# Two passes over the feed-forward slices become three, and VectorE takes the casts of q, k, v and x

## The chip, the cores and the metric

One core of one Trainium2 chip runs the whole program in one launch. The metric is the device time of that launch in microseconds (us). The core has TensorE for matmuls (PE, its weight loads are PEld), VectorE (DVE), ScalarE (ACT) and GpSimd (POOL); SyncE (SP) issues every DMA here. Each engine works through its own list of instructions in a fixed order and waits where an operand isn't there yet.

## The reference

```python
def phi(x):                                   # q and k: 8 batches, 8 heads, 576 tokens, 64 wide
    proj = x @ w_phi                          # 64 -> 128 features
    proj = proj - max(abs(proj), axis=-1)     # one number for each token
    return concat([exp(proj), exp(-proj)])    # 256 features
q_p, k_p = phi(q), phi(k)
kv = k_p.T @ v                                # (256, 64) for each head
z = k_p.sum(tokens)
x = (q_p @ kv) / (q_p @ z + 1e-6)             # heads side by side: 4608 tokens, 512 wide
out = ((x @ w_a) * (x @ w_b)) @ w_out         # 512 -> 1536 -> 512
```

q, k, v and w_phi are float32; the three feed-forward weights are 64-bit floats.

## The kernel before

**Number formats.** A float32 matmul costs TensorE several passes over its columns. The kernel therefore splits most operands into a high part in `float32r` (`hi`, a cast) and a low part (`lo`, source minus high part) and adds three products, hi·hi + hi·lo + lo·hi. The helper `split` issues the cast on one engine and the subtraction on VectorE. The first head pairs of the program are "plain": their float32 operands go to TensorE unsplit. `PLAIN_K, PLAIN_Q, PLAIN_KV, PLAIN_NUM` say up to which of the 32 pairs this holds in the k projection, the q projection, the product of features and v, and the numerator.

**Attention.** Heads go in 32 pairs. A pair has four chunks of 128 tokens and half a chunk that it shares with its neighbour. `features` projects a chunk of k: the tokens are the weights of the matmul and the feature matrix streams past in 256 columns. Plain pairs stream a block-diagonal matrix `wk32`, so that one matmul does both heads. Split pairs stack high part and low part of one head in the 128 rows (`stack`), which takes one matmul for each head and chunk, and then a copy `kb` on ScalarE and an add `kd` on VectorE to join the halves (L236, L237). The absolute maximum (`m`), the subtraction (`kd`), two exponentials (`ke`) and the split `keh`, `kel` follow; `kv_add` accumulates `kvps`. `k_finish` transposes `kvps`. `q_side` does the same for q with features on partitions: projection `pq`, copy to `p`, an all-reduce of the absolute maximum over partitions on GpSimd (L350), subtraction, exponentials `qe`, split `qeh`, `qel`, and the numerator matmuls `pn` with the denominator as 65th row. Numerators go to DRAM (`xun`), denominators are inverted (`reciprocals`) and go to DRAM as `rec`.

**Feed-forward.** The 1536 inner columns are 12 slices of 128. Pass one (`moe_block`) does 6 slices for 16 blocks of 288 tokens and writes partial sums to `part` in DRAM. A block's x is the product of `xun` and `rec` (L533), split into `xh`, `xl`. Pass two (`second_pass`, `winograd`) does the other 6 slices for 9 blocks of 512 tokens, two slices and four quarters of 128 rows of x at a time, with seven products in place of eight; it needs sums of weights (`load_factors`) and sums of x (`factors_of_x`) that VectorE makes. It adds `part` and writes the output. The 64-bit weights are decoded on ScalarE and VectorE (`decode`).

**Order of the work.** `attention_steps` gives every step of a pair a turn; after each turn `run(work, int(due))` lets steps of feed-forward blocks run, `PACE0` and later `PACE` steps a turn, so that their matmuls fill TensorE while attention goes on. When the turns are over, 5 blocks of pass one are left (`BLOCKS_LAST`); beside them the weights of pass two are made. A timeline scheduler then sets the final order on each engine. PSUM has 8 banks: `ps_moe` 3, attention 4 and `kvacc` 1; after attention `ps_late` has 5 beside `ps_moe`.

Of the kernel before, what the change touches and what calls it, by code (L numbers as in the profile page):

```python
# [59 lines left out]
def tile_kernel(ctx, tc, qT, km, kr, vm, vr, w_phi, w_a, w_b, w_out, out):  # L60
# [95 lines left out]
    def k_load(b, pr, a1, a2, ps, consts, st):  # L156
# [4 lines left out]
        if i < PLAIN_K:  # L161
            k32 = a1.tile([P, n], F32, tag="ks", bufs=2, name=f"k32_{u}")
            nc.sync.dma_start(k32, km[b, pr])
        else:
            k32 = a1.tile([P, 2, n], F32, tag="k32", name=f"k32_{u}")
            for r in range(2):
                nc.sync.dma_start(k32[r * D : (r + 1) * D], km[b, pr].rearrange("(j d) s -> d j s", j=2))
# [21 lines left out]
    def rest_load(b, g, a1, a2, ps, consts, st):  # L189
# [3 lines left out]
        if i < PLAIN_K:  # L193
            k32 = a1.tile([P, P], F32, tag="rk32", name=f"rk32_{u}")
            nc.sync.dma_start(k32, kr[b, g])
        else:
            k32 = a1.tile([P, 2, P], F32, tag="rk32", name=f"rk32_{u}")
            for r in range(2):
                nc.sync.dma_start(k32[r * D : (r + 1) * D], kr[b, g].rearrange("(j d) s -> d j s", j=2))
# [18 lines left out]
    def features(u, i, k_, c0, n, a2, ps, consts):  # L218

        wk32, wk2 = consts[3:5]  # L220
        d = a2.tile([P, 4, F], F32, tag="kd", bufs=1, name=f"kd_{u}")[:, : 2 * n]
        if i < PLAIN_K:
            pk = ps.tile([P, 2, 2 * F], F32, tag="att", name=f"pk_{u}")
            for c in range(n):
                nc.tensor.matmul(pk[:, c], k_[:, (c0 + c) * P : (c0 + c + 1) * P], wk32, start=True, stop=True)
# [616 lines left out]
```

## Time and profile before

| what | value |
|---|---|
| median of 3 runs | 1262.51 us (1260.01 to 1264.18) |
| profiled execution, span from first to last instruction | 1260.6 us |
| granted TensorE clock, mean | 0.998 |
| TensorE busy | 1229.8 us (98%) |
| VectorE busy | 928.8 us (74%) |
| ScalarE busy | 734.3 us (58%) |
| GpSimd busy | 157.3 us (12%) |
| DMA | 138.24 MB, mean 110 GB/s |

The page gives no time of its own for the profiled execution beside the span; the three runs lie within 3.6 us of that span. TensorE's busy share overstates its use, since the matmuls overlap in the records; how far apart they start tells what one costs. The page's slices show TensorE and VectorE both well filled until about 680 us, where attention ends, and VectorE half idle after it.

### The profile page before, as it was taken

The page shows a single profiled execution, that of the slowest core. Times are in us where ns is not written, and L with a number is a line of the kernel's source. Part 1 is how long each engine was busy: PE and PEld are TensorE (multiplying, and loading weights), DVE is VectorE, ACT ScalarE, POOL GpSimd, SP SyncE. Part 2 cuts the span into 40 slices and gives each one's busy share as a digit, 9 for nine tenths or more (in the row PEclk, how much of TensorE's full clock was granted, in tenths as well). Part 3 has the DMA queues.
Part 4 walks back from the last instruction along what each step waited for, and adds up shares of the span by engine and source line. Part 5 has one row for each costly group of instructions (what it writes and reads, how often), then busy time and mean ns, then how long its engine had stood idle before and what let it go on. Part 6 is the DMA issues. An engine that isn't in the chain of part 4 may idle for free.

```text
span 1260.6 us, 22965 instructions
## 1 busy us (share of the span) xinstructions
PE 1229.8 (98%) x8588; PEld 1131.8 (90%) x8588; DVE 928.8 (74%) x1682; ACT 734.3 (58%) x1577; POOL 157.3 (12%) x70
## 2 busy tenths in 40 slices
PE   7889999999999999999999999999999999999998
PEld 4556789899999999999999999999999999999997
DVE  6989658898898989989974983599556556456443
ACT  5766668788888889988885542454223223233221
POOL 2232221221222212221220000000000000000000
PEclk9999999999999999999999999999999999999999
DMA  7665443443444435344233561142432332331221
GB/s 188 174 182 154 117 125 90 108 128 103 122 110 123 127 101 141 81 129 130 62 82 104 166 204 58 46 146 83 125 94 70 107 101 67 101 103 51 66 68 50
DMA packets 126287, 138.24 MB, mean 110 GB/s; under 512 B 39712, under 2 KB 92448, under 8 KB 126176
## 3 DMA queue, kind: packets, MB, share of 16 engines
q1 hardware_dynamic: 126176, 136.78, 38.4%
q8 instruction: 67, 1.10, 0.4%
q14 instruction: 44, 0.36, 0.1%
HBM read 108.12 MB, written 28.61 MB: 108 GB/s over the span
## 4 chain that ended last, share of the span: by engine, by line
PE 76%; DVE 9%; DMA 6%; ACT 5%; issue 2%; SPq 1%; POOL 0%; DVEq 0%; ACTq 0%
PE pab L648 21%; PE po L695 11%; PE pa L565 10%; PE pb L565 10%; PE po L588 9%; PE kvps L292 6%; PE pn L370 5%; PE pq L346 2%; DMA raw_b<-in_w_b 1%; PE pk L234 1%; DVE qs L154 1%; DMA rb<-rec 1%; DMA r<-den 1%; DVE kd L240 1%; DVE kel L149 1%
## 5 line engine op out<-in xcount | busy, mean ns | idle before, releaser
L350 POOL PARTITION_ALL_REDUCE mb<-p x64 | 156.6, 2448 | 495.9 <-ACT p L347 465.8
L565 PE MATMUL pb<-xh,wh_b 128*128 128x288 f32 x384 | 114.9, 299 | 2.9 <-ACT h L569 2.9
L565 PE MATMUL pa<-xh,wh_a 128*128 128x288 f32 x384 | 115.5, 301 | 0.4 <-ACT o L591 0.2
L565 PE MATMUL pb<-xh,wl_b 128*128 128x288 f32 x384 | 114.5, 298 | 0.0
L565 PE MATMUL pa<-xh,wl_a 128*128 128x288 f32 x384 | 114.4, 298 | 0.0
L142 ACT CAST hh<-h 128x288 fp32r<-128x288 f32 (+1 forms) x150 | 72.7, 503 | 70.7 <-DVE h L570 40.7
L565 PE MATMUL pa<-xl,wh_a 128*128 128x288 f32 x384 | 113.2, 295 | 0.0
L565 PE MATMUL pb<-xl,wh_b 128*128 128x288 f32 x384 | 112.7, 293 | 0.0
L588 PE MATMUL po<-hh,wl_o 128*128 128x288 f32 x384 | 112.4, 297 | 0.0
L588 PE MATMUL po<-hl,wh_o 128*128 128x288 f32 x384 | 111.9, 295 | 0.3 <-DVE hl L149 0.3
L588 PE MATMUL po<-hh,wh_o 128*128 128x288 f32 x384 | 110.3, 298 | 0.6 <-DVE h L570 0.6
L149 DVE TENSOR_TENSOR hl<-h,hh 128x288 fp32r<-128x288 f32 (+1 forms) x150 | 81.2, 554 | 22.7 <-ACT hh L142 22.5
L695 PE MATMUL po<-hl,wh_o 128*128 128x512 f32 x216 | 84.5, 391 | 0.0
L695 PE MATMUL po<-hh,wl_o 128*128 128x512 f32 x216 | 84.3, 390 | 0.0
L533 DVE TENSOR_TENSOR x<-x,rb 128x288 f32<-128x288 f32 (+1 forms) x100 | 56.0, 564 | 37.8 <-DMA x<-xun 26.2
L695 PE MATMUL po<-hh,wh_o 128*128 128x512 f32 x216 | 79.2, 392 | 0.0
L565 PEld LDWEIGHTS pb<-xh,wh_b 128*128 128x128 f32 x384 | 72.2, 188 | 5.0 <-ACT h L569 3.9
L565 PEld LDWEIGHTS pa<-xh,wh_a 128*128 128x128 f32 x384 | 72.2, 188 | 3.8 <-issue 2.3
L588 PEld LDWEIGHTS po<-hl,wh_o 128*128 128x128 f32 x384 | 72.5, 189 | 1.1 <-DVE hl L149 0.7
L565 PEld LDWEIGHTS pa<-xl,wh_a 128*128 128x128 f32 x384 | 72.9, 190 | 0.6 <-issue 0.2
L565 PEld LDWEIGHTS pa<-xh,wl_a 128*128 128x128 f32 x384 | 72.1, 188 | 1.3 <-issue 1.1
L565 PEld LDWEIGHTS pb<-xl,wh_b 128*128 128x128 f32 x384 | 72.8, 190 | 0.3
(226 smaller groups left out, 3793.7 us busy)
## 6 DMA issues: line engine op xcount, KB each, us to landing
q<-in_qT SPq DMA_DIRECT2D x110, 144.0 KB
k<-in_km SPq DMA_DIRECT2D x55, 256.0 KB
xun<-xn SPq DMA_DIRECT2D x64, 144.0 KB
x<-xun SPq DMA_DIRECT2D x64, 144.0 KB
rb<-rec SPq DMA_DIRECT2D x128, 72.0 KB
part<-o SPq DMA_DIRECT2D x16, 576.0 KB
o<-part SPq DMA_DIRECT2D x36, 256.0 KB
out_x<-o SPq DMA_DIRECT2D x36, 256.0 KB
```

The costliest lines, as they stand in the source:

```text
L142: eng.copy(dst, src)
L149: eng_lo.tensor_tensor(lo, src, hi, op=ALU.subtract)
L154: eng_lo.tensor_tensor(hi_lo[D:], src[D:], hi_lo[D:], op=ALU.subtract)
L292: nc.tensor.matmul(st["kv_ps", b, pr][:width, j], v_[:, j, :width], e_[:, j], start=(left == NFULL and j == 0 and n_ == 0), stop=(left == ...
L346: nc.tensor.matmul(pq[:, :HALF], w_, q_[:, tok], start=(n_ == 0), stop=(n_ == len(parts) - 1))
L350: nc.gpsimd.partition_all_reduce(mb, p32, P, bass_isa.ReduceOp.absmax)
L370: nc.tensor.matmul(pn[: D + 1, :HALF], kv_[:, 2 * j + s, :], e_[:, s, tok], **at)
L533: nc.vector.tensor_tensor(x32, x32, rb, op=ALU.mult)
L565: nc.tensor.matmul(acc, w[:, cc * P : (cc + 1) * P], x, start=(k == 0), stop=(k == 3 * NCC - 1))
L588: nc.tensor.matmul(acc, w[:, cc * P : (cc + 1) * P], h, start=(k == 0), stop=(k == 3 * NFS[p] - 1))
L648: nc.tensor.matmul(acc[to][:, i], w_, x_, skip_group_check=True, **at)
L695: nc.tensor.matmul(acc[cc], w[:, cc * P : (cc + 1) * P], h, **at)
```

## The change

Three passes of 4 slices take the place of two of 6. Pass one runs in 9 blocks of 512 tokens, and the other two passes both use the seven-product form, with two groups of two slices for each block (`later_passes`). Pass one writes its normalised x to DRAM (`xnorm`), and the later passes read that in place of `xun` and `rec`. The weights of pass three are made during pass two; those that have no room are written to DRAM (`keep`) and fetched into the places of pass two's weights behind its last block (`fetch`).

In attention the split k projection uses the block-diagonal form: three matmuls of 256 columns for each chunk, and no join. The first 5 pairs are plain in place of 9 (7 in place of 11 for `kvps`). The casts of k, v, q and x go from ScalarE to VectorE. The tiles `qs`, `qe`, `qeh`, `qel` and `kd` have two buffers. `k_finish` is cut into two steps. PSUM is 2 banks for `ps_moe`, 5 for attention and 1 for `kvacc`, and later 6 + 2.

```diff
-PACE0, PACE, PACE0_UNTIL = 0.65, 0.9, 18
+PACE0, PACE, PACE0_UNTIL = 0.6, 0.62, 18
-PLAIN_K, PLAIN_Q, PLAIN_KV, PLAIN_NUM = 9, 9, 11, 9
+PLAIN_K, PLAIN_Q, PLAIN_KV, PLAIN_NUM = 5, 5, 7, 5
-    "k_hi": "vss",
+    "k_hi": "vvv",
-    "v_hi": "sss",
+    "v_hi": "vvv",
-    "q_hi": "vss",
+    "q_hi": "vvv",
-SLICES0 = 6
-T2 = 512
-BLOCKS_LAST, AHEAD = 5, 0.7
+SLICES = (4, 4, 4)
+T1, T2 = 512, 512
+BLOCKS_LAST, AHEAD, LATER = 2, 2.5, 0.75
+LATE, EXTRA = 19, 7
...
-    ps_moe = ctx.enter_context(tc.tile_pool(name="ps_moe", bufs=3, space=PSUM))
+    ps_moe = ctx.enter_context(tc.tile_pool(name="ps_moe", bufs=2, space=PSUM))
-    part = dpool.tile([DM, NT], F32, name="part")
+    parts = [dpool.tile([DM, NT], F32, name=f"part{i}") for i in range(2)]
+    xnorm = dpool.tile([DM, NT], F32, name="xnorm")
-        ps = c.enter_context(tc.tile_pool(name="ps_att", bufs=4, space=PSUM))
+        ps = c.enter_context(tc.tile_pool(name="ps_att", bufs=5, space=PSUM))
...
 # k_load
-            ks = a1.tile([P, 2, n], F32R, tag="ks", bufs=2, name=f"ks_{u}")
-            stack(ks, k32, engine("k_hi", b), engine("k_lo", b))
+            kh, kl = (a1.tile([P, n], F32R, tag=f"k{p}", bufs=2, name=f"k{p}_{u}") for p in "hl")
+            split(kh, kl, k32, engine("k_hi", b), engine("k_lo", b))
...
 # features
-            for c in range(n):
-                pk = ps.tile([P, 2, 2, F], F32, tag="att", name=f"pk_{u}_{c}")
-                for j in range(2):
-                    nc.tensor.matmul(pk[:, j], k_[:, j, (c0 + c) * P : (c0 + c + 1) * P], wk2, start=True, stop=True)
-                to = slice(2 * c, 2 * c + 2)
-                nc.scalar.copy(kb[:, to], pk[:, :, 1])
-                nc.vector.tensor_tensor(d[:, to], pk[:, :, 0], kb[:, to], op=ALU.add)
+        parts = products(k_, (wk32,) if len(k_) == 1 else wks)
+        for c in range(n):
+            tok = slice((c0 + c) * P, (c0 + c + 1) * P)
+            for n_, (x_, w_) in enumerate(parts):
+                at = dict(start=(c == n_ == 0), stop=(n_ == len(parts) - 1))
+                nc.tensor.matmul(pk[:, c], x_[:, tok], w_, skip_group_check=True, **at)
...
 # load_x
-            split(xh, xl, x32, nc.scalar, nc.vector)
+            split(xh, xl, x32, nc.vector, nc.vector)
...
+    def put(key, shape, places, stored):
+        name = "_".join(map(str, key))
+        if stored is None:
+            pool, tag = slots[key] = places.popleft()
+            return pool.tile(shape, F32R, tag=tag, name=f"w_{name}")
+        fetches[key] = dpool.tile(shape, F32, name=f"wd_{name}")
+        return stored["pool"].tile(shape, F32R, tag="stage", bufs=2, name=f"ws_{name}")
+    def fetch(key, place):
+        pool, tag = place
+        t = pool.tile(list(fetches[key].shape), F32R, tag=tag, name="w_" + "_".join(map(str, key)))
+        nc.sync.dma_start(t.bitcast(F32), fetches[key])
+        weights[key] = t
...
 # moe_block, pass one
+            if f == 1:
+                for c, x_ in enumerate(xs):
+                    nc.sync.dma_start(xnorm[c * P : (c + 1) * P, j * T : (j + 1) * T], x_[2])
...
 # factors_of_x, passes two and three
-            x = [x_chunk(1, j, cc, pool, 4) for cc in (c, c + NCC // 2)]
+            for i in range(2):
+                cc = c + i * NCC // 2
+                nc.sync.dma_start(x[i], xnorm[cc * P : (cc + 1) * P, j * T2 : (j + 1) * T2])
...
-    def second_pass(xin):
+    def later_passes(xin, after):
+        blocks = [(p, j) for p in (1, 2) for j in range(NT // T2)]
+        for at, (p, j) in enumerate(blocks):
+            dst = out if p == 2 else parts[1]
...
+    ahead, due = all_weights(2, {"pool": extra}), 0.0
+    for _ in second:
+        ahead_by(LATER)
```

The order of the instructions moves with it at two places that matter. The first is VectorE in the middle of attention, beside the first two chunks of pair 1 of batch 4. `kd` is the projection of k, `kel` and `qel` are low parts of exponentials, `qs` the stacked q, `kvl` the low part of `kv`, `x32` and `xh` the x of a block of pass one. Before:

```order
L533 TENSOR_TENSOR x32_0_5_0_5446<-x32_0_5_0_5446,rb_0_5_0_5447 128x288
L381 TENSOR_SCALAR r_3_2_3816<-r_3_2_3816 128x9
L382 RECIPROCAL r_3_2_3816<-r_3_2_3816 128x9
L237 TENSOR_TENSOR kd_4_1_0_3824<-pk_4_1_0_0_3826,kb_4_1_0_3825 128x256
L237 TENSOR_TENSOR kd_4_1_0_3824<-pk_4_1_0_1_3831,kb_4_1_0_3825 128x256
L149 TENSOR_TENSOR kel_4_0_r_3925<-ke_4_0_r_3921,keh_4_0_r_3924 128x512
L239 TENSOR_REDUCE m_4_1_0_3836<-kd_4_1_0_3824 128x4
L533 TENSOR_TENSOR x32_0_5_1_5456<-x32_0_5_1_5456,rb_0_5_1_5457 128x288
L240 TENSOR_TENSOR kd_4_1_0_3824<-kd_4_1_0_3824,m_4_1_0_3836 128x512
```

The same place of the changed kernel, with its casts on VectorE:

```order
L223 TENSOR_REDUCE m_4_1_0_3574<-pk_4_1_0_3567 128x4
L193 MEMSET rv32_4_1_3490 128x2
L151 TENSOR_TENSOR qel_3_7_3603<-qe_3_7_3599,qeh_3_7_3602 128x1152
L306 TENSOR_TENSOR kvl_3_3_3561<-pt_3_3_3554,kvh_3_3_3559 128x260
L151 TENSOR_TENSOR hl_0_2_2_3663<-h32_0_2_2_3659,hh_0_2_2_3662 128x512
L146 CAST xh_0_3_0_4304<-x32_0_3_0_4295 128x512
L366 TENSOR_SCALAR r_3_2_3549<-r_3_2_3549 128x9
L224 TENSOR_TENSOR kd_4_1_0_3566<-pk_4_1_0_3567,m_4_1_0_3574 128x512
L146 CAST xh_0_3_1_4317<-x32_0_3_1_4308 128x512
L146 CAST qs_4_3_3925<-q32_4_3_3775 128x576
```

The two adds ahead of the maximum are gone, the maximum reads PSUM, and casts of x and q stand between the steps of k.

The second place is TensorE at the same chunks: `pk` is the projection of k, `pn` the numerator, `po`, `pa` and `pb` belong to a block of pass one, `pt` is the transpose of `kvps`. Before:

```order
L370 MATMUL pn_3_5_1_3806<-qeh_3_5_3551,kvl_3_2_3402 65x288 x2
L234 MATMUL pk_4_1_0_0_3826<-wk2_111,ks_4_1_3660 128x256 x2
L588 MATMUL po_0_3_2_4380<-hh_0_3_5_4174,wh_0_5_o_885 128x288
L234 MATMUL pk_4_1_0_1_3831<-wk2_111,ks_4_1_3660 128x256 x2
L588 MATMUL po_0_3_0_4225<-hl_0_3_5_4175,wh_0_5_o_885 128x288
L588 MATMUL po_0_3_0_4225<-hh_0_3_5_4174,wl_0_5_o_886 128x288
```

The same place of the changed kernel:

```order
L299 MATMUL pt_3_3_3554<-ident_121,kvT_3_3_3454 128x65 x4
L220 MATMUL pk_4_1_0_3567<-wkh_110,kh_4_1_3432 128x256
L220 MATMUL pk_4_1_0_3567<-wkl_111,kh_4_1_3432 128x256
L220 MATMUL pk_4_1_0_3567<-wkh_110,kl_4_1_3433 128x256
L220 MATMUL pk_4_1_0_3567<-wkh_110,kh_4_1_3432 128x256
L220 MATMUL pk_4_1_0_3567<-wkl_111,kh_4_1_3432 128x256
L220 MATMUL pk_4_1_0_3567<-wkh_110,kl_4_1_3433 128x256
L580 MATMUL pa_0_2_3_3706<-xh_0_2_0_3272,w_0_3_a_h_453 128x512
```

Four matmuls for two chunks have become six, and the matmuls of the block beside them are 512 columns wide.

More of the change, by code (lines that the diff above doesn't have):

```diff
@@ L160, in k_load @@
         n = NFULL * P
[L161 to L167, printed above, removed]
+        k32 = a1.tile([P, n], F32, tag="k32", bufs=2, name=f"k32_{u}")
+        nc.sync.dma_start(k32, km[b, pr])
         if i < PLAIN_KV:
@@ L192, in rest_load @@
         i = b * NPAIR + 2 * g
[L193 to L199, printed above, removed]
+        k32 = a1.tile([P, P], F32, tag="rk32", name=f"rk32_{u}")
+        nc.sync.dma_start(k32, kr[b, g])
         v32 = a1.tile([P, 2, D + 1], F32, tag="rv32", name=f"rv32_{u}")
@@ L205, in rest_load @@
         if i >= PLAIN_K:
-            ks = a1.tile([P, 2, P], F32R, tag="rk", name=f"rk_{u}")
-            stack(ks, k32, engine("k_hi", b), engine("k_lo", b))
-            st["rk", b, g] = (ks,)
+            kh, kl = (a1.tile([P, P], F32R, tag=f"rk{p}", name=f"rk{p}_{u}") for p in "hl")
+            split(kh, kl, k32, engine("k_hi", b), engine("k_lo", b))
+            st["rk", b, g] = (kh, kl)
         yield
@@ L352, in q_side @@
         yield
-        e = a2.tile([P, 2, S], F32, tag="qeh" if plain else "qe", bufs=1, name=f"qe_{u}")
+        e = a2.tile([P, 2, S], F32, tag="qeh" if plain else "qe", bufs=2, name=f"qe_{u}")
         nc.scalar.activation(e[:, 0], p32, AF.Exp)
@@ L464, in load_weights @@
             s, g = yield from decode(load_raw(p, f, nm, stage), u, stage)
-            hi, lo = (
-                pool.tile([P, DM], F32R, tag=tag, name=f"w{part}_{u}")
-                for part, (pool, tag) in zip("hl", place or ((wpool, f"wh_{f}_{nm}"), (wpool, f"wl_{f}_{nm}")))
-            )
+            if places is not None and stored is None:
+                while len(places) < 2:
+                    yield
+            own = places if places is not None else deque((wpool, f"w{part}_{f}_{nm}") for part in "hl")
+            hi, lo = (put((p, f, nm, part), [P, DM], own, stored) for part in "hl")
             nc.scalar.copy(hi, s)
@@ L673, in winograd @@
         for i in range(2):
[L674 removed]
+            hl = [pool.tile([P, 2, n], F32R, tag=f"h{part}", bufs=NFS[1], name=f"h{part}_{u}_{i}") for part in "hl"]
             split(*hl, h32[i], nc.scalar, nc.vector)
@@ L713, in second_pass @@
                 next(quads[q])
+                after(p, j, q)
                 yield
-            if cols.stop < NT:
-                xs = yield from factors_of_x(j + 1, xin)
+            if at + 1 < len(blocks):
+                xs = yield from factors_of_x(*blocks[at + 1], xin)
             early = range(2 * nq - 2)
@@ L750, in tile_kernel @@
                 at = turn + BLOCK_LAG
-                tasks[at] = [moe_block(0, ready * per + h) for h in range(per)]
+                done = (ready + 1) * S // TS[0]
+                tasks[at] = [moe_block(j) for j in range(blocks, done)]
+                blocks = done
             for t in sorted(tasks):
```

245 lines of the change are left out of this document (126 added, 119 removed).

## The prediction, on record before the changed kernel ran

> **What bounds the kernel now.** I read the page's header first, then the stages, then the distances between matmuls.
>
> ```profile
> span 1260.6 us, 22965 instructions
> PE 1229.8 (98%) x8588; PEld 1131.8 (90%) x8588; DVE 928.8 (74%) x1682; ACT 734.3 (58%) x1577; POOL 157.3 (12%) x70
> DVE  6989658898898989989974983599556556456443
> ```
>
> TensorE is busy nearly always, VectorE on average at three quarters, but the slices show it at eight or nine tenths until attention ends and at half after. The last attention matmul gives the border, and the windows the two sides of it; columns are length, PE, PEld, DVE, ACT, POOL, clock, DMA share, GB/s.
>
> ```profile
> L370 PE MATMUL pn<-qeh,kvl x184: 288/294/344, 198.0 to 681.0; 128*65 128x288 f32 x184
> ...
> 0.00:150.00 150.00, 132.99 (x610) 85.44 (x611) 120.46 (x234) 98.30 (x213) 43.11 (x23) 0.99 0.61 165
> 150.00:681.30 531.30, 524.40 (x3922) 501.56 (x3921) 459.86 (x758) 445.89 (x962) 114.18 (x47) 1.00 0.40 108
> 681.30:1260.60 579.30, 572.43 (x4061) 544.76 (x4060) 348.44 (x692) 190.11 (x403) 0.00 (x0) 1.00 0.32 97
> ...
> 500.00:550.00 50.00, 50.00 (x386) 49.00 (x386) 47.39 (x79) 44.91 (x98) 10.83 (x5) 1.00 0.45 122
> ```
>
> Attention with its filling takes 681.3 us, the rest 579.3 us. In the first part VectorE is busy 120.5 + 459.9 = 580.3 us, 85% of it, and up to 94.8% over 50 us. The TensorE clock is full in both. Busy time overlaps for matmuls, so I price them by runs of the chain of work that ended last (start, length, engine, tile, count).
>
> ```profile
> 120.82 1.73 PE kvps L292 x8
> 128.78 1.94 PE pn L370 x8
> 739.04 9.54 PE po L588 x72
> 1002.76 4.11 PE po L695 x18
> 1008.95 2.88 PE pab L648 x24
> 1049.44 4.11 PE po L695 x18
> ```
>
> That gives 9.54/72 = 132.5 ns for 288 split columns, 4.11/18 = 228.3 ns for 512 and 2.88/24 = 120 ns for 256. A plain float32 matmul leaves two records: 1.73/4 = 432 ns for 256 columns, 1.94/4 = 485 ns for 288. A block of pass two takes 1049.44 − 1002.76 = 46.68 us, and 252 x 0.120 + 72 x 0.2283 = 46.68: its matmuls stand back to back.
>
> **TensorE's sum, part by part.** Pass one: 16 blocks of 216 matmuls at 132.5 ns are 457.9 us; 9 blocks of 144 at 228.3 ns are 295.9 us. Passes of the seven-product form: 9 x 46.68 = 420.1 us become 18 x (168 x 0.120 + 48 x 0.2283) = 18 x 31.12 = 560.2 us. Feed-forward goes from 878.0 to 856.1 us, −21.9.
>
> In attention I counted the matmuls in the order of both programs. Split ones of 256 columns go from 830 to 1107 (three for two in the k projection, and four more split pairs), split ones of 288 from 736 to 864, plain ones from 153 + 108 to 95 + 60. At the prices above: 99.6 + 97.5 + 66.2 + 52.4 = 315.7 us before, 132.8 + 114.5 + 41.1 + 29.1 = 317.5 us after, +1.8; 128 transposes at some 60 ns (7.7 us) stay. The k projection pays for what the fewer plain pairs save. TensorE's total is 1201.4 us now and 1181.3 us then, −20.1.
>
> **Where this work lies.** Ahead of the last `pn` stand 2311 feed-forward matmuls of 288 columns before and 960 of 512 after. So the attention stage holds 306.2 + 323.4 = 629.6 us of TensorE work before, against 681.3 us of time: 51.7 us lost. After, it holds 219.2 + 325.2 = 544.4 us. The rest holds 151.7 + 420.1 = 571.8 us before, 7.5 us less than its 579.3, and 76.7 + 560.2 = 636.9 us after. So 85 us of TensorE work leaves the first stage, and 65 us arrives in the second.
>
> **VectorE in the first stage.** It doesn't shrink with TensorE's share. These rows price its part.
>
> ```profile
> L237 DVE TENSOR_TENSOR kd<-pk,kb 128x256 f32<-128x256 f32 x92 | 35.5, 415 | 7.4 <-ACT kb L236 6.5 <-ACT ke_r L249 0.5
> L154 DVE TENSOR_TENSOR ks<-k,ks 64x1024 fp32r<-64x1024 f32 x23 | 28.1, 1223 | 0.7
> L149 DVE TENSOR_TENSOR qel<-qe,qeh 128x1152 fp32r<-128x1152 f32 x46 | 63.0, 1370 | 11.0 <-ACT qeh L142 10.8
> L149 DVE TENSOR_TENSOR kel<-ke,keh 128x1024 fp32r<-128x1024 f32 x42 | 51.1, 1217 | 0.9 <-ACT keh L142 0.7
> L149 DVE TENSOR_TENSOR vl<-v,vaug x21: 676/684/1789, 178.8 to 626.0; 128x512 fp32r<-128x512 f32 x21
> L149 DVE TENSOR_TENSOR xfl<-x,xfh x18: 415/424/426, 718.9 to 1180.4; 128x256 fp32r<-128x256 f32 x18
> L117 DVE CAST wh<-w x1: 226/226/226, 3.6 to 3.6; 128x128 fp32r<-128x128 f32 x1
> L118 DVE TENSOR_TENSOR wl<-w,wh x1: 291/291/291, 4.1 to 4.1; 128x128 fp32r<-128x128 f32 x1
> L439 DVE TENSOR_SCALAR w_q_a<-w_q_a x6: 418/420/427, 690.6 to 823.0; 128x512 uint32<-128x512 uint32 x6
> ```
>
> Two-operand work costs about 1.04 ns a column over a fixed 155 (291, 424, 684, 1217 ns at 128, 256, 512, 1024). Casts of 512 columns stand nowhere before. The bounds are the single-operand row of the same width, 420 ns, and the two-operand row, 684 ns; the one cast of 128 columns, 226 beside 291 ns, sides with the lower, as does 226 + 384 x 0.52 = 426 from its own kind. I take 420, and 450 for 576 columns.
>
> Gone: the joins (92 x 0.415 and 11 of the half chunks, 40 us), the stacked k (28 + 5 us for the half chunks), 6 of 18 weight decodes (22 us), and some 23 us of `h`, `x` and their splits, since pass one does 960 x 512 columns there and not 2311 x 288. Together −118 us. Added: k casts and splits 27 x (0.420 + 0.684) = 30 us and 6 for half chunks, casts of v 25 x 0.420 + 2.6 = 13, of q 54 x 0.450 = 24, of x 28 x 0.420 = 12, and the splits of four more pairs (8 `qel`, 8 `kel`, 8 `qs`, 4 `vl` and the small ones) 32. Together +117 us. VectorE stays at 580 us. At the upper bound for casts it would be 134 x 0.26 = 35 us more.
>
> ScalarE loses the `kb` copies, the casts of k, q, v and x, and a third of the decoding.
>
> ```profile
> L236 ACT COPY kb<-pk 128x256 f32<-128x256 f32 x92 | 31.5, 383 | 2.8 <-PE pk L234 2.8
> L142 ACT CAST qs<-q 128x576 fp32r<-128x576 f32 x46 | 32.0, 697 | 0.8 <-DMA q<-in_qT 0.8
> L142 ACT CAST ks<-k 128x1024 fp32r<-128x1024 f32 x23 | 24.6, 1069 | 1.2 <-PE pk L225 1.2
> ```
>
> These three alone are 88 us of its 98.3 + 445.9 = 544 us, so it no longer matters. So VectorE must fit 580 us beside 544 us of TensorE work. With a loss like the present one (51.7), TensorE alone would end the stage at 596 us; VectorE would have to be busy 97% of it. It can get denser: operations that follow at once start before the last one's record ends.
>
> ```profile
> 694.14 0.68 DVE L441 SCALAR_TENSOR_TENSOR w_q_a<-raw_a,w_q_a 128x512 uint32<-128x512 uint32 x1
> 694.74 0.69 DVE L483 TENSOR_TENSOR w_q_a<-w_q_a 128x512 f32<-128x512 f32 x1
> 695.35 0.42 DVE L442 TENSOR_SCALAR w_q_a<-w_q_a 128x512 uint32<-128x512 uint32 x1
> ```
>
> Here 0.60 us apart for 0.68 recorded: 80 ns each. If an eighth of its 935 instructions, those that stand behind an idle today, follow at once, busy time falls by about 10 us, to 570. At the 94.8% of its best window that is 601 us for the stage: the value I take. Its ends are 580/0.948 = 612 with no gain in density, and 585 if two buffers for `qs`, `qe` and `kd`, the fifth PSUM bank and six fewer weight loads take away part of the early loss.
>
> **The second stage.** 636.9 us of matmuls plus the present loss of 7.5 us, plus 4 us for two new seams. At the end of attention two blocks are left, not five: 76.7 us of TensorE work instead of 151.7 us cover the first weight factors. VectorE needs for them 2 x (4 x 0.684 + 2 x 0.684 + 4 x 0.420 + 11 x 0.424) = 21 us, 8 us for sums and splits of x, and some 20 us for the blocks: 49 of 76.7, so covered; if VectorE comes out of attention 30 us behind, the seam opens. At a block's end the early output matmuls that cover the last product's chain fall from 24 to 12 (5.5 to 2.7 us).
>
> ```profile
> L670 DVE TENSOR_TENSOR h<-top 128x512 f32<-128x512 f32 x27 | 18.6, 689 | 0.5
> L142 ACT CAST hh<-h 128x512 fp32r<-128x512 f32 x54 | 30.8, 620 | 29.5 <-DVE h L670 29.5
> L149 DVE TENSOR_TENSOR hl<-h,hh 128x512 fp32r<-128x512 f32 x54 | 35.4, 687 | 13.1 <-ACT hh L142 13.1
> ```
>
> That chain is an add of 0.69, 0.69 + 0.62 + 0.69 = 2.7 us, just covered, and the order puts products of the next block there too. Between nothing and 0.7 us in 18 blocks, 0 to 12 us, I take 4 for both seams. The traffic grows (`xnorm` and a second partial sum written and read, 22 factors stored and fetched) by about 40 MB, or 32 GB/s on 97 to 108, where the first window carried 165: no cost, and none for SyncE's 97 more rows, unless a store that waits for VectorE holds up a load of x behind it; x is issued a block ahead, which covers 31 us. PSUM's ring for pass one falls from three banks to two: an accumulator is reused after 12 x 0.2283 = 2.7 us of the other's matmuls instead of 2 x 1.6 us, which leaves `h` two to three VectorE operations of slack.
>
> **The sum.** 601 + 636.9 + 7.5 + 4 = 1249.4 us against the profiled 1260.6: −11.2. The span is 1.9 us under the median of the runs, 1262.5, so I forecast 1251 us. The stage may last 612 us before nothing is gained.
>
> **The rivals.**
> - TensorE keeps the bound and the early loss shrinks: the stage ends at 585, total 1233 + 2 = 1235 us. For it: ScalarE is relieved and the double buffers loosen the chains. Against it: VectorE would be busy 97 to 99%.
> - VectorE takes over and runs less densely, the rival on the other side. In the first 150 us it is at 120.5/150 = 80%, where chains and loads decide, and the split pairs now begin there. With 127 us of its work at 80% and the other 450 at 92%: 159 + 489 = 648 us, total 1298 us; at 95% in the second part 633 us and 1283 us. It decides from a share of 580/612 = 94.8% downwards. For it: in-order queues, two nearly equal engines. Against it: today's idle of VectorE is largely waiting for TensorE.
> - The seams cost 12 to 18 us instead of 4: 1259 to 1265 us, no change.
> [...]
>
> ```profile
> L350 POOL PARTITION_ALL_REDUCE mb<-p x64: 2141/2293/4374, 18.4 to 659.2; - x64
> L154 DVE TENSOR_TENSOR qs<-q,qs x46: 755/756/1741, 150.3 to 650.6; 64x576 fp32r<-64x576 f32 x46
> ```
>
> A `qs` split takes 756 ns or, during an all-reduce, up to 985 ns more, well under the 2293 ns of an all-reduce. There are 64 all-reduces before and after, and 580 us holds today's delays. If the 134 new casts were delayed by 985 ns as often as GpSimd is busy in the stage, 157/681 = 23%, that is 30 us more on VectorE: 610/0.948 = 643 us, 1293 us. If all-reduces that delay something already merely delay a cast instead, nothing is added; a third of the 30 us would bring 1262.
>
> [...]
>
> **How the numbers follow.** Changes under 0.3% (3.8 us) can't be told from none here. Chances: my forecast 0.43 (1242 to 1262, of it 0.37 faster and 0.06 the same), TensorE keeps the bound 0.18 (faster), VectorE less dense 0.23 (0.20 slower, 0.03 the same), the seams 0.09 (0.05 the same, 0.04 slower), the port 0.07 (0.04 slower, 0.03 the same). Faster 0.55, same 0.17, slower 0.28. The range 1231 to 1282 leaves out the better half-tenth of the second case and the worse half of the third; the forecast's own is 1242 to 1262.
>
> **What would show it.** Right: last `pn` near 601 us, VectorE at about 95% from 150 us on, casts of 512 columns at 420 ns, blocks of passes two and three 31.1 us apart, blocks of pass one alone 32.9 us. Wrong: TensorE idle behind VectorE's `kel`, `qel`, `h` over some 68 us before the last `pn`; casts near 680 ns; a gap at the first or the tenth block of the seven-product form.

## The result, and the profile after

The changed kernel takes 1275.19 us (median; 1272.50 to 1277.42) against 1261.26 us (1260.01 to 1264.18) for the kernel before in the same rounds: a ratio of 1.0106, 95% interval 1.0081 to 1.0130, some 13.5 us slower. The forecast was 1251 us. The profiled execution has a span of 1275.0 us (before: 1260.6).

The header, two rows of slices and the shares of the chain that ended last, from the page after:

```profile
span 1275.0 us, 20737 instructions
PE 1226.1 (96%) x7593; PEld 1067.4 (84%) x7593; DVE 1033.3 (81%) x1845; ACT 674.1 (53%) x1305; POOL 162.3 (13%) x70
DVE  6999999999999999996698998957556565656553
PEclk8999999999999999999989999999999999999999
...
PE 61%; DVE 25%; DMA 6%; issue 5%; ACT 2%; SPq 2%; POOL 0%; DVEq 0%; ACTq 0%
```

VectorE now shows nine tenths from the second to the eighteenth slice (32 to 574 us), where it showed five to nine before. It makes up 25% of the chain that ended last, against 9% before. One slice behind attention (638 to 669 us) has a TensorE clock of eight tenths. The border and the stages, as rows of the group of `pn` and of the windows (length, PE, PEld, DVE, ACT, POOL, clock, DMA share, GB/s):

```profile
L355 PE MATMUL pn<-qeh,kvl x216: 288/294/502, 107.2 to 613.7; 128*65 128x288 f32 x108
...
0.00:150.00 150.00, 131.12 (x606) 88.92 (x607) 136.44 (x249) 98.48 (x199) 41.06 (x23) 0.97 0.59 168
150.00:613.90 463.90, 449.54 (x2766) 388.61 (x2765) 442.88 (x698) 335.81 (x629) 121.28 (x47) 1.00 0.44 127
613.90:1275.00 661.10, 645.39 (x4225) 589.87 (x4224) 453.98 (x901) 239.82 (x477) 0.00 (x0) 0.99 0.41 134
```

The attention stage ends at 613.9 us instead of 681.3 (forecast 601), the rest takes 661.1 us instead of 579.3 (forecast 648.4). So 67 us were won in the first stage and 82 lost in the second, of which 65 are the planned matmuls. VectorE's busy time in the stage, 136.4 + 442.9 = 579.3 us, is 94.4% of it.

What happens behind attention stands in the timelines around 613 to 647 us (start, length, engine, line, tile, idle time before and what ended it): first TensorE, then VectorE's rows for the x of block seven, then SyncE's queue.

```profile
629.42 0.39 PE L580 MATMUL pb<-xl,w_b_h 128*128 128x512 f32 x1
629.65 0.40 PE L580 MATMUL pb<-xh,w_b_l 128*128 128x512 f32 x1
638.27 0.79 PE L580 MATMUL pa<-xh,w_a_h 128*128 128x512 f32 x1 [8.22 <-DVE xh L146]
...
640.54 0.80 PE L580 MATMUL pa<-xl,w_a_h 128*128 128x512 f32 x1 [1.06 <-DVE xl L151]
...
645.17 0.63 PE L580 MATMUL pa<-xh,w_a_h 128*128 128x512 f32 x1
645.60 0.63 PE L580 MATMUL pa<-xl,w_a_h 128*128 128x512 f32 x1
...
647.20 0.40 PE L580 MATMUL pb<-xh,w_b_h 128*128 128x512 f32 x1
647.43 0.39 PE L580 MATMUL pb<-xl,w_b_h 128*128 128x512 f32 x1
```

```profile
620.16 0.69 DVE L545 TENSOR_TENSOR x<-x,rb 128x512 f32<-128x512 f32 x1 [4.58 <-DMA rb<-rec]
621.10 0.17 DVE L366 TENSOR_SCALAR r<-r 128x9 f32<-128x9 f32 x1 [0.24 <-DMA r<-den]
621.31 0.22 DVE L367 RECIPROCAL r<-r 128x9 f32<-128x9 f32 x1
...
634.19 1.28 DVE L545 TENSOR_TENSOR x<-x,rb 128x512 f32<-128x512 f32 x2
...
637.80 0.41 DVE L146 CAST xh<-x 128x512 fp32r<-128x512 f32 x1
```

```profile
619.38 0.37 SPq L365 DMA_DIRECT2D r<-den  x1
...
621.55 0.34 SPq L368 DMA_DIRECT2D rec<-r  x1
621.93 0.43 SPq L606 DMA_DIRECT2D part<-o  x1
622.41 2.27 SPq L617 DMA_DIRECT2D x<-xnorm  x3
624.72 0.90 SPq L543 DMA_DIRECT2D rb<-rec  x1
```

The last `pn` starts at 613.7 us. Its denominators are fetched at 619.4, the reciprocals written at 621.6, broadcast (`rb`) from 624.7 on, behind loads for the next pass; VectorE, whose list has weight decoding and sums of x in between, multiplies at 634.2 and casts at 637.8. TensorE had work until 630.0 and stands 8.2 us, then another 1.1. After the hole its matmuls of 512 columns start 0.43 us apart until 646.45 and then 0.23 again. The granted clock was 0.50 from 634 to 646.5 us and 1.00 from 646.5 to 680: the half clock lasted 8.2 us after the restart, in which TensorE once waited again.

Passes two and three run as priced. In the chain of work that ended last, the same group of output matmuls two blocks apart:

```profile
1152.65 5.47 PE po L709 x24
...
1214.89 5.47 PE po L709 x24
```

(1214.89 − 1152.65)/2 = 31.12 us for a block, as the prediction had it.

### The profile page after: what moved, and what is told of

Same layout as the page of the kernel before. It is cut to its first block, busy times and chain, and to the rows that moved or that the text cites. A ratio compares the mean times of both kernels' runs of the same rounds, so it can differ in the third digit from the quotient of the medians.

```text
span 1275.0 us, 20737 instructions
## 1 busy us (share of the span) xinstructions
PE 1226.1 (96%) x7593; PEld 1067.4 (84%) x7593; DVE 1033.3 (81%) x1845; ACT 674.1 (53%) x1305; POOL 162.3 (13%) x70
## 4 chain that ended last, share of the span: by engine, by line
PE 61%; DVE 25%; DMA 6%; issue 5%; ACT 2%; SPq 2%; POOL 0%; DVEq 0%; ACTq 0%
PE pab L659 27%; PE po L709 15%; PE po L601 4%; PE pa L580 3%; PE pb L580 3%; PE kvps L276 3%; DVE kel L151 2%; PE pn L355 2%; DVE qel L151 2%; DVE p L336 2%; DVE qs L156 2%; DVE m L223 2%; DVE kd L224 2%; DMA rb<-rec 1%; DVE qs L146 1%
## 5 line engine op out<-in xcount | busy, mean ns | idle before, releaser
L709 PE MATMUL po<-hl,w_o_h 128*128 128x512 f32 x288 | 113.7, 395 | 0.0
L709 PE MATMUL po<-hh,w_o_l 128*128 128x512 f32 x288 | 113.1, 393 | 0.0
L709 PE MATMUL po<-hh,w_o_h 128*128 128x512 f32 x288 | 109.4, 395 | 2.5 <-ACT hh L144 2.2
L659 PE MATMUL pab<-xth,w_b_s 128*128 128x256 f32 x432 | 95.3, 283 | 0.0
L659 PE MATMUL pab<-xth,w_a_s 128*128 128x256 f32 x432 | 94.6, 282 | 0.0
L144 ACT CAST hh<-h 128x512 fp32r<-128x512 f32 x108 | 63.8, 619 | 50.4 <-DVE h L585 29.0
L151 DVE TENSOR_TENSOR qel<-qe,qeh 128x1152 fp32r<-128x1152 f32 x54 | 76.9, 1423 | 4.8 <-ACT qeh L144 4.5
L151 DVE TENSOR_TENSOR hl<-h,hh 128x512 fp32r<-128x512 f32 x108 | 71.6, 682 | 7.2 <-ACT hh L144 7.0
L659 PEld LDWEIGHTS pab<-xth,w_b_s 128*128 128x128 f32 x432 | 75.1, 192 | 0.7
L659 PEld LDWEIGHTS pab<-xth,w_a_s 128*128 128x128 f32 x432 | 73.8, 191 | 2.0
L339 ACT ACTIVATE qe<-p 128x576 f32<-128x576 f32 x64 | 44.1, 689 | 40.7 <-DVE p L336 39.1
L232 ACT ACTIVATE ke<-kd 128x512 f32<-128x512 f32 x64 | 40.5, 634 | 44.8 <-DVE kd L224 44.1
```

The lines of the kernel that those rows point to most:

```text
L144: eng.copy(dst, src)
L151: eng_lo.tensor_tensor(lo, src, hi, op=ALU.subtract)
L232: nc.scalar.activation(e[:, :, 0, :], d, AF.Exp)
L339: nc.scalar.activation(e[:, 0], p32, AF.Exp)
L659: nc.tensor.matmul(acc[to][:, i], w_, x_, skip_group_check=True, **at)
L709: nc.tensor.matmul(acc[cc], w[:, cc * P : (cc + 1) * P], h, **n_)
```

## The experiments

All ratios are against the kernel before, run beside each kernel. Where two experiments are compared, it is by these ratios, times 1261 us. "Last `pn`" is where the attention stage ends in the profiled execution, and "behind it" counts the matmuls of pass one that come after it in that trace. Two borders can be compared only with as many matmuls behind them: one more or less moves the border by 0.233 us (0.1325 us in e3, whose matmuls are those of the kernel before, which has 1145 behind its last `pn`).

| run | edit of the changed kernel | time, us | ratio, 95% interval | last `pn`, us | behind it |
|---|---|---|---|---|---|
| the changed kernel | | 1275.2 | 1.0106 (1.0081 to 1.0130) | 613.7 | 336 |
| e1 | casts of k, q, v, x back on ScalarE | 1292.5 | 1.0232 (1.0211 to 1.0253) | 630.6 | 347 |
| e2 | x of the last batch from batch 6 | 1266.2 | 1.0030 (1.0017 to 1.0042) | 613.6 | 338 |
| e3 | (the kernel before) casts on VectorE | 1279.5 | 1.0127 (1.0104 to 1.0149) | 737.0 | 864 |
| e4 | nine plain pairs again | 1289.1 | 1.0211 (1.0191 to 1.0230) | 622.5 | 327 |
| e5 | cast of q twice | 1290.7 | 1.0226 (1.0194 to 1.0258) | 622.9 | 360 |
| e6 | no lower half of `qs` | 1251.9 | 0.9916 (0.9886 to 0.9946) | 588.6 | 348 |
| e7 | two k products, not three | 1270.4 | 1.0071 (1.0045 to 1.0096) | 605.4 | 338 |
| e8 | every x from the batch before | 1262.1 | 1.0006 (0.9991 to 1.0020) | 628.0 | 261 |
| e9 | casts of v on ScalarE | 1269.2 | 1.0064 (1.0040 to 1.0089) | 603.9 | 348 |
| e10 | v's low part on GpSimd | 1363.0 | 1.0814 (1.0792 to 1.0836) | 698.6 | 338 |
| e11 | e1 with every x from the batch before | 1262.6 | 1.0024 (1.0006 to 1.0041) | 609.8 | 336 |
| e12 | e9 and e10 together | 1396.5 | 1.1075 (1.1050 to 1.1101) | 733.6 | 338 |
| e13 | last two blocks by chunks of x | 1263.1 | 1.0021 (1.0011 to 1.0031) | 613.6 | 336 |
| e14 | e13 and e9 | 1255.1 | 0.9955 (0.9937 to 0.9974) | 604.0 | 348 |
| e15 | single buffers again | 1312.9 | 1.0409 (1.0377 to 1.0441) | 647.1 | 290 |
| e16 | PSUM 3 + 4 + 1 again | 1284.5 | 1.0186 (1.0169 to 1.0203) | 623.5 | 334 |

**Which engine sets the stage: e5, e6, e7.**

e5:

```diff
+            copy(engine("q_hi", b), qs, q32)
             stack(qs, q32, engine("q_hi", b), nc.vector)
```

> The changed kernel with the cast of q on VectorE issued twice (54 x 0.447 = 24 us more on VectorE in the attention stage; same values, same TensorE work). Theory A, VectorE sets the length of the stage: 579 + 24 = 603 us of VectorE at its share of 94.4% is a stage of 639 us, 25 us longer, about 1300 us in all. Theory B, TensorE with the waits of the chains in both engines' fixed lists sets it, VectorE's load only in part: 5 to 10 us longer, 1280 to 1285 us.

e6:

```diff
-            stack(qs, q32, engine("q_hi", b), nc.vector)
+            copy(engine("q_hi", b), qs, q32)
```

> The changed kernel without the subtraction that makes the lower half of qs (54 x 0.756 = 41 us less on VectorE, q's low parts are left out; TensorE's work is the same). Theory A, VectorE sets the stage: 538 us of it at 94.4% would be 570 us, so TensorE's work with the loss it had before the change (544 + 52) takes over, a stage of 596 us, 18 us shorter, about 1257 us. Theory B, TensorE with the waits in the fixed lists: the stage stays within 6 us of 614 us, 1269 to 1277 us.

e7:

```diff
-        parts = products(k_, (wk32,) if len(k_) == 1 else wks)
+        parts = products(k_, (wk32,) if len(k_) == 1 else wks)[:2]
```

> The changed kernel with two products instead of three in the k projection (the one of k's low part with the weights' high part is left out, about 230 matmuls of 256 columns, 27.6 us of TensorE work in the attention stage; VectorE's work is the same). Theory A, VectorE sets the stage: it stays within 5 us of 614 us, the time at 1272 to 1278 us. Theory B, TensorE's work with the waits of the chains: the stage is 20 to 28 us shorter, 1247 to 1255 us.

The border in each, by the last group of `pn` (e5, e6, e7):

```profile
L356 PE MATMUL pn<-qeh,kvl x216: 288/294/503, 108.6 to 622.9; 128*65 128x288 f32 x108
```

```profile
L355 PE MATMUL pn<-qeh,kvl x216: 288/294/442, 101.6 to 588.6; 128*65 128x288 f32 x108
```

```profile
L355 PE MATMUL pn<-qeh,kvl x216: 289/295/504, 105.5 to 605.4; 128*65 128x288 f32 x108
```

Doubling the cast cost 15 us of time, between theory B (5 to 10) and theory A (25). Leaving out the lower half took 24 us off, more than the 18 of A, and B wanted none. e7 was sized wrongly in its expectation: with four chunks a pair the program loses 121 matmuls, 121 x 0.120 = 14.5 us, not 27.6. It gained 4.4 us, and the stage became 8 us shorter: 2 and 4 us below theory A's ranges, and far from B. VectorE's busy time over the whole run, 1033.3 us in the changed kernel, is 1054.4 us in e5 and 981.3 in e6. So a microsecond of VectorE's work is worth 15/21 = 0.7 us in e5 and 24/52 = 0.5 us in e6, one of TensorE's 4.4/14.5 = 0.3. VectorE's load is what the stage follows most, but it isn't alone. e5 and e6 also lengthen and shorten the chain from q to `pq`, so load and latency aren't separated here.

**The hole behind attention: e2, e8, e13, e14.** e2 and e8 read x of another batch, so that no x waits for its reciprocal: e2 for the last batch alone, e8 for all. e13 computes everything.

In `x_chunk`, e2 and then e8:

```diff
             n = min(S - s0, (j + 1) * T - t)
+            b = min(b, B - 2)
```

> The changed kernel, but the two blocks of pass one that need the last batch take their x from batch 6: the numerators and reciprocals of batch 7 are still made and stored, and nobody reads them. It takes away the chain from the last numerator to the x of those blocks. Theory A (this chain opens the 8 us hole at 630 us, and the hole brings 14 us of TensorE at half its clock): the hole and the half clock go, the last matmul of attention stays near 614 us, and the total falls by 12 to 17 us to about 1260 us. Rival B (VectorE's backlog of weight decoding and x opens the hole): a hole of 5 us or more stays before the last two blocks and the total falls by less than 6 us.

```diff
             n = min(S - s0, (j + 1) * T - t)
+            b = max(b - 1, 0)
```

> The changed kernel with x of every block of pass one taken from the batch before its own (numerators and reciprocals of the right batch are left unread), so that no x waits for a reciprocal. Theory A, VectorE's load sets the stage: it stays at 614 us and only the hole behind the attention goes, 1264 to 1267 us as with the last batch alone. Theory B, the waits of x for the DMA of rb at the head of VectorE's list hold the attention up: the stage is 8 to 20 us shorter too, 1245 to 1257 us.

e13, in `moe_block`; the banks are chosen after the first `yield`, so that block seven too has the late ones:

```diff
-        psum = pools_moe[-1]
         yield
+        psum, pabs = pools_moe[-1], {}
...
-            for nm in ("a", "b"):
-                acc = psum.tile([P, T], F32, tag="moe", name=f"p{nm}_{u}")
...
+            if f not in pabs:
+                late = psum is not ps_moe and f == 0
+                fs = range(3) if late else (f,)
+                pabs.update((g, {nm: psum.tile([P, T], F32, tag="moe", name=f"p{nm}_{p}_{j}_{g}") for nm in "ab"}) for g in fs)
+                accs = [(cc, g, nm) for cc in range(NCC) for g in fs for nm in "ab"]
+                for cc, g, nm in accs if late else sorted(accs, key=lambda a: a[2]):
...
+            pab = pabs[f]
```

> The changed kernel, all of the computation in place, with the last two blocks of pass one in another order: the first three slices' accumulators in six late PSUM banks, chunk of x by chunk, so that 54 matmuls and not 18 (12.4 us, not 4.1) need only the first three chunks, whose x is there before the last pair's reciprocals. Theory A, the hole behind attention and the half clock after it cost 9 to 11 us: they go, 1263 to 1267 us. Theory B, x of the last batch came early in the earlier run and that gave the time by other ways: 1271 to 1276 us.

e14 is e13 and, in `ENGINES`:

```diff
-    "v_hi": "vvv",
+    "v_hi": "sss",
```

> The same order of the last two blocks, and the casts of v on ScalarE. Theory A, the gains add up (9 to 11 us of the hole, 6 us of VectorE): 1257 to 1261 us, equal to the kernel before or a little faster. Theory B, they overlap: 1264 to 1270 us.

The rest of e2 and of e13 in the windows, one row of each:

```profile
613.80:1263.60 649.80, 642.58 (x4227) 588.31 (x4226) 452.81 (x898) 239.47 (x478) 0.00 (x0) 1.00 0.42 134
```

```profile
613.80:1261.10 647.30, 640.40 (x4225) 586.85 (x4224) 453.53 (x900) 239.12 (x477) 0.00 (x0) 1.00 0.42 136
```

In both the stage ends where it did, and the rest falls from 661.1 to 649.8 and 647.3 us at full clock. e2 gained 9.6 us of time, less than the 12 to 17 of its theory A and more than the 6 of B; e13 gained 10.7, as its theory A had it. In e13 the last chunk is no earlier, but TensorE has 54 matmuls for the first three chunks in front of it; two rows of its timeline, the last of those and the next wait:

```profile
637.34 0.40 PE L582 MATMUL pb<-xh,w_b_l 128*128 128x512 f32 x1
637.70 0.50 PE L582 MATMUL pa<-xh,w_a_h 128*128 128x512 f32 x1
...
639.98 0.50 PE L582 MATMUL pa<-xl,w_a_h 128*128 128x512 f32 x1 [0.61 <-DVE xl L151]
```

e8 gained 12.6 us, 3 more than e2. Its order differs (261 matmuls of pass one stand behind the last `pn`, not 336): 628.0 − 75 x 0.2333 = 610.5 us is the border to compare, 3 us less. Its time lies 2 us below theory A's range and 5 us above B's: x's wait for the reciprocals holds up the stage of the changed kernel by 3 us at most. e14 adds the cast of v to e13:

```profile
604.20:1257.00 652.80, 644.68 (x4237) 590.40 (x4235) 457.02 (x906) 239.19 (x478) 0.00 (x0) 1.00 0.42 136
```

The gains of e13 and e9 (5.3 us, below) add up: 16 us by the two alone, 19 measured. At 1255.1 us e14 is 0.45% faster than the kernel before and 1.5% faster than the changed one. It is the fastest version here that does the whole computation.

**The casts back on ScalarE: e1, e11, e9, e3.**

e1:

```diff
-    "k_hi": "vvv",
+    "k_hi": "vss",
...
-    "v_hi": "vvv",
+    "v_hi": "sss",
...
-    "q_hi": "vvv",
+    "q_hi": "vss",
...
-            split(xh, xl, x32, nc.vector, nc.vector)
+            split(xh, xl, x32, nc.scalar, nc.vector)
```

> The changed kernel, with the casts of k, v, q and x on ScalarE again and nothing else undone. Theory A (VectorE bounds attention, 579 us busy of 614): VectorE's list up to the last split of the exponentials loses 63 us of priced work, so attention ends near 590 us, by TensorE's 541 us of work plus some 48 us of loss, and the total falls by about 24 us to 1251 us; VectorE's share of the stage drops to about 89%. Rival B (the latency of chains or the two PSUM banks of pass one bound attention, VectorE is only full because it is late): the stage stays at 610 to 618 us and the total within 5 us of 1275 us. Rival C (ScalarE becomes the bound with 597 us of priced work, about 510 us without overlap): the stage ends above 600 us and ScalarE is busy over 90% of it.

e11 is e1 with the line of e8:

> The kernel with all casts back on ScalarE (1292 us) and x of every block taken from the batch before its own, so that no x waits for a reciprocal (right numerators are left unread). With the casts on VectorE the same edit gave 13 us. Theory D, in the kernel with the casts back it is the 52 us of VectorE's waits for the DMA of rb that make it slow: 25 to 40 us less, 1252 to 1267 us. Theory C, it is the casts that ScalarE makes late: only the hole behind the attention goes, 10 to 15 us, 1277 to 1282 us.

e9 is the changed kernel with the line of e14 alone:

> The changed kernel with the casts of v alone back on ScalarE (25 x 0.42 us and the small ones, 13 us less on VectorE, about as much more on ScalarE). Theory A, each us of VectorE's work in the attention stage is worth 0.6 us of time, as the doubled cast of q and the missing lower half of qs gave: 8 us less, 1264 to 1270 us. Theory C, a split that goes through both engines costs more by its hand-over than VectorE saves, which would be why all casts together on ScalarE were slower: 1275 to 1283 us.

e3 is the kernel before with e1's edit the other way round (k, v, q "vvv", the cast of x on `nc.vector`):

> The kernel before, with the casts of k, v, q and x on VectorE and nothing else changed: one part of the change alone. Its VectorE has about 70 us of idle in attention. Theory A (a cast on VectorE costs what its row says, 420 ns for 512 columns, and matters only when VectorE is full): VectorE is busy about 650 us up to the last numerator, 92 to 94% of the stage, TensorE stays the bound, and the total is within 8 us of 1261 us. [...]

e1 missed what each theory said of it: slower by 16 us, the stage 17 us longer, with VectorE down to 519 us in it. The waits of VectorE (what it waited for, in total, times, longest) tell where: first in the changed kernel, then e1, then e11.

```profile
DVE x L545 <- DMA rb<-rec: 13.1, 5, 4.6
```

```profile
DVE x L545 <- DMA rb<-rec: 52.0, 23, 6.3
```

```profile
DVE x L546 <- DMA rb<-rec: 19.2, 11, 4.5
```

With its casts gone VectorE reaches `x` earlier than the broadcast reciprocals land, and everything behind it in the list waits too. e11 takes most of that wait away (52.0 us fall to 19.2), on other data, and the kernel gains 26 us, theory D. At 1.0024 it is then within 2.3 us of e8, the same with the casts on VectorE. So without the waits of x it makes little difference which of the two engines casts; e11's windows have both nearly equally full:

```profile
150.00:610.00 460.00, 449.74 (x2790) 393.54 (x2789) 400.25 (x571) 402.67 (x778) 114.43 (x48) 0.99 0.45 128
```

VectorE 87%, ScalarE 87.5%. Between the ends lies e9: 14 us of casts moved (VectorE's total falls from 1033.3 to 1019.3 us), 5.3 us gained, theory A.

In e3 the casts alone cost the kernel before 16 us, twice what theory A allowed. The border at 737.0 us is no measure of that: 281 matmuls fewer lie behind it, 37 us, so the stage grew by 19 us and not by 56. VectorE is busy 654 us of it, 89% and not the 92 to 94% of theory A. The casts of 512 columns took 448 ns in the mean, and the all-reduces 2434 ns against 2448. What grew are the delays beside all-reduces. A VectorE operation counts here as delayed when its record is over 0.2 us longer than the median of its kind. Added up from the traces, these excesses are 50.3 us in the kernel before and 65.4 in e3; in the changed kernel they are 58.2 us, and 43.3 in e1. Every one of these operations overlaps an all-reduce. So both pairs of runs say that the casts on VectorE bring 15 us of delays with them. What these 15 us cost in time, no run shows.

**GpSimd instead: e10, e12.**

e10, and e12 with the line of e14 besides:

```diff
-    "v_lo": "vvv",
+    "v_lo": "ppp",
...
-        return {"v": nc.vector, "s": nc.scalar}[ENGINES[step][min(b, 2)]]
+        return {"v": nc.vector, "s": nc.scalar, "p": nc.gpsimd}[ENGINES[step][min(b, 2)]]
```

> The changed kernel with the subtraction that makes v's low part on GpSimd (25 x 0.684 us, 17 us less on VectorE; GpSimd is busy 26% of the stage). Theory A, 0.6 us for each us of VectorE: 10 us less, 1262 to 1268 us. [...]

> The changed kernel with the casts of v on ScalarE and the subtraction for v's low part on GpSimd, so that v's split leaves VectorE (30 us less). Theory A, 0.6 us for each us of VectorE: 18 us less, about 1257 us, faster than the kernel before. [...]

Both lost 90 to 120 us against the changed kernel, where theory A had gains of 10 and 18. GpSimd's timeline in e10:

```profile
308.67 4.80 POOL L335 PARTITION_ALL_REDUCE mb<-p  x2 [6.24 <-DVE kh L146]
320.32 1.94 POOL L151 TENSOR_TENSOR vl<-v,vaug 128x512 fp32r<-128x512 f32 x1 [6.85 <-PE pa L580]
328.62 2.28 POOL L335 PARTITION_ALL_REDUCE mb<-p  x1 [6.36 <-ACT hh L144]
335.15 2.14 POOL L335 PARTITION_ALL_REDUCE mb<-p  x1 [4.25 <-DVE rkh L146]
344.78 1.54 POOL L151 TENSOR_TENSOR vl<-v,vaug 128x512 fp32r<-128x512 f32 x1 [7.49 <-DVE p L336]
```

Each time that the kind of work changes, GpSimd is idle first, for 5.8 to 8.3 us in all 54 changes of e10, mostly put down to work that `vl` and `mb` don't read. Two all-reduces in a row can follow at once (308.67, x2). The subtraction itself takes 1.5 us. The loss lies in the stage, 85 and 120 us longer, and VectorE's wait for the all-reduces shows the way it takes. In e10:

```profile
DVE p L336 <- POOL mb L335: 48.6, 11, 8.5
```

In e12 it is 109.0 us, and 1.5 in the changed kernel. Part of the loss may come by TensorE's clock, whose mean falls to 0.968 and 0.952 (0.988 in the changed kernel); how much, no run shows. What GpSimd does in the pauses, the rows don't show either.

**The other parts of the change: e4, e15, e16.**

e4:

```diff
-PLAIN_K, PLAIN_Q, PLAIN_KV, PLAIN_NUM = 5, 5, 7, 5
+PLAIN_K, PLAIN_Q, PLAIN_KV, PLAIN_NUM = 9, 9, 11, 9
```

> The changed kernel, with as many plain pairs as the kernel before (9, 9, 11, 9). VectorE loses 41 us of priced work in attention, TensorE gains 13 us there and 11 us in all. Theory A (VectorE bounds attention): the stage falls from 614 us to about 600 us and the total by 8 to 16 us to 1259 to 1267 us although TensorE has more to do. Rival B (TensorE's work and chains bound attention): the stage grows by 10 us and the total to 1285 us.

e15 has `bufs=1` for the tags kd, ke, qs, qe, qeh and qel, in the way of this line (the change had given `ke` a second buffer too):

```diff
-            qs = a2.tile([P, S], F32R, tag="qs", bufs=2, name=f"qs_{u}")
+            qs = a2.tile([P, S], F32R, tag="qs", bufs=1, name=f"qs_{u}")
```

> The changed kernel with one buffer each for d, e, qs, and q's e and its two halves, as before the change. Theory A, VectorE's load sets the stage and a chain that waits for a buffer is covered: within 5 us of 1275 us. Theory B, TensorE and VectorE waited for these buffers and the second one is worth what I counted on: 10 to 25 us slower, 1285 to 1300 us.

e16 (and `spare` gives three of "moe" for the first batch):

```diff
-    ps_moe = ctx.enter_context(tc.tile_pool(name="ps_moe", bufs=2, space=PSUM))
+    ps_moe = ctx.enter_context(tc.tile_pool(name="ps_moe", bufs=3, space=PSUM))
...
-        ps = c.enter_context(tc.tile_pool(name="ps_att", bufs=5, space=PSUM))
+        ps = c.enter_context(tc.tile_pool(name="ps_att", bufs=4, space=PSUM))
...
-    pools_moe.append(ctx.enter_context(tc.tile_pool(name="ps_late", bufs=6, space=PSUM)))
+    pools_moe.append(ctx.enter_context(tc.tile_pool(name="ps_late", bufs=5, space=PSUM)))
```

> The changed kernel with PSUM divided as before (three banks for pass one, four for attention, one for kv; five late banks). Theory A, neither ring limits the stage: within 4 us of 1275 us. Theory B, two banks hold up pass one: 5 to 12 us faster, 1263 to 1270 us. Theory C, the fifth attention bank is a gain: 5 to 15 us slower.

All three parts are gains within the change: without them the kernel is 13, 38 and 10 us slower. ScalarE's wait ahead of q's exponentials, in the changed kernel and in e15, shows what the buffers do:

```profile
ACT qe L339 <- DVE p L336: 39.1, 27, 3.1
```

```profile
ACT qe L339 <- DVE qel L151: 54.1, 34, 4.5
```

With two buffers ScalarE waits for its input; with one it waits until VectorE's last reader of the buffer is done, and the two engines take turns. The hole grows too: TensorE waits 19.4 us in one piece for `xh` behind attention. In e16 it is the exponentials of k:

```profile
ACT ke L232 <- DVE kd L224: 68.0, 34, 6.7
```

against 44.1 us in the changed kernel, as it would be if `pk` came later with four banks; no run shows that. e4 shows the limit of "VectorE sets the stage": it takes 38 us off VectorE in the stage (541.6 us) and adds 13 us to TensorE by the prices of the prediction, and the stage becomes 9 us longer, 7 with as many matmuls behind the border. The plain pairs all lie in the first 190 us. TensorE's largest wait in the stage of the changed kernel is not for VectorE either, but for ScalarE's `kvh`, 4.9 us before the change; no run takes it away alone.

```profile
PE pn L355 <- ACT kvh L302: 10.3, 10, 2.3
```

## Why the prediction was wrong

- **TensorE's sum** held: the blocks of passes two and three at 31.12 us, the rest without its hole (e13) 647.3 us against the forecast 636.9 + 7.5 + 4 = 648.4. A small miss lies in pass one, whose matmuls of 512 columns start 2.80/12 = 233 ns apart and not 228: 1296 x 5 ns = 6 us in all, most of it in the stage.

```profile
650.16 2.80 PE pa L580 x12
652.96 2.80 PE pb L580 x12
```

- **VectorE's priced work** held, with casts of 512 columns at 419 ns. The recorded times of its operations up to the last `pn`, added up, are 636.1 us before and 643.2 after; without the delays beside all-reduces they fall by 0.8 us, and the prediction's terms (−118 and +117) by 1. Rows after, the groups of x's casts and of both halves of `qs` (the last two with busy time and mean ns, then idle time):

```profile
L146 DVE CAST xh<-x x36: 406/419/1518, 54.5 to 663.6; 128x512 fp32r<-128x512 f32 x36
L156 DVE TENSOR_TENSOR qs<-q,qs 64x576 fp32r<-64x576 f32 x54 | 44.2, 819 | 1.7
L146 DVE CAST qs<-q 128x576 fp32r<-128x576 f32 x54 | 28.7, 532 | 1.5 <-DMA q<-in_qT 1.4
```

- **The delays beside all-reduces**, "the port" of the chances, stood at nothing in the sum and grew by 7.9 us: 50.3 us in 56 operations became 58.2 us in 78. That a port causes them, no run shows; the traces show that all of these operations overlap an all-reduce. Part of the delays only moved, the way out that this rival named: the cast of q takes 532 ns in the mean against the 450 that I took, while the subtraction behind it fell to 819 from this, in the kernel before:

```profile
L154 DVE TENSOR_TENSOR qs<-q,qs 64x576 fp32r<-64x576 f32 x46 | 49.0, 1066 | 10.7 <-ACT qs L142 8.9 <-DMA rv<-in_vr 0.7
```

But with 64 all-reduces in both kernels, 56 delayed one operation each before; after, 42 delayed one and 18 delayed two. And the 985 ns that this rival was priced with is the longest delay of `qs` alone: the prediction's own row of `vl`, 684 ns in the median and 1789 at most, has 1105.
- **The step that failed first** is VectorE's busy time, "busy time falls by about 10 us, to 570", and in it the delays put at nothing. The overlap that was to bring the fall did come: neighbouring records overlap by 64.0 us in the stage against 56.1, a gain of 7.9 us. The 7.9 us of new delays took it back, and busy time stayed at 579.3 us. That it equals the 580 of the first estimate is chance, two changes that cancel. At 94.8% the 9.3 us missing are 10 us of the 12.9 missed in the stage; the rest is the share, 94.4%. The nearest of the recorded cases is the mildest of these delays, a third of the 30 us. The break-even of 612 us, worked out for a stage without a gain in busy time, was the better value. e5 and e6 bear out that the stage follows VectorE; how much of it follows the order of the lists (e4, e11) stays open.
- **The best window** of 94.8% is no limit either, and that the share came out beside it is partly luck. The same window after the change:

```profile
500.00:550.00 50.00, 49.27 (x310) 42.72 (x309) 49.66 (x80) 36.86 (x70) 12.35 (x5) 1.00 0.42 117
```

VectorE is busy 99% of it and 98% from 150 to 550 us. The stage loses its share at the ends: 40.0 of the first 50 us, 50.3 of the last 63.7.
- **The step that failed second** is "4 us for both seams". Behind attention the rest lost 661.1 − 636.9 − 7.5 = 16.7 us, the rival's 12 to 18. I had looked for the seam at the first weight factors and at VectorE's backlog. It lay in the chain from the last `pn` over denominators, reciprocals and their broadcast to `x`, and I had not asked which of the remaining blocks need the last batch: with two blocks left both do, with five before only two. The half clock after the hole, 0.43 instead of 0.23 us a matmul, wasn't in the sum at all.
- **The range** of 1231 to 1282 us held the time. My case for "slower" asked for one large mishap; what came were two rivals in a mild form, the delays beside all-reduces in the stage and the seam at its price, 12.9 + 12.7 us together.

## What to carry to other kernels

When work moves to an engine that already fills a stage, add to its own rows what delays it there: here the delays beside GpSimd's all-reduces grew by 8 us and took back what a denser list had gained. When less work is left to cover a seam, follow the last producer's whole chain, its DMA hops and its place in each in-order list, and ask of each remaining block which of its inputs hang on it; an accumulation ordered by input chunks can fill the wait with work that is there already. Moving a step to a less busy engine helps in small pieces (14 us of casts gained 5), and can lose when what it freed only waits at the head of a list.

## What the runs showed of the hardware

- After 8.2 us without a matmul TensorE ran at a granted clock of 0.50 for 8.2 us more: 0.43 us for 512 columns, 0.23 behind that (the changed kernel).
- GpSimd paused 5.8 to 8.3 us at each of 54 changes between an all-reduce and an elementwise subtraction (e10).
- VectorE operations beside an all-reduce of GpSimd (2.5 us in the mean) took up to 1.14 us longer than the median of their kind. In the kernels before and after, all 56 and all 78 operations that were over 0.2 us too long overlapped one.
- Matmuls of 512 columns in pass one start 233 ns apart, those of the later passes 5.47/24 = 228 ns, with the same shapes; no run shows the cause.
